# The position bias of the middle query chunks, computed per distance and written out in both directions

## Chip, core and metric

One core of one Trainium2 chip. The metric is the device time of one execution in microseconds. TensorE is called PE, VectorE DVE, ScalarE ACT, GpSimd POOL; SP is the engine that only issues transfers.

## The reference

Attention with a learned position bias, followed by two gated MLPs, all in float32:

```python
B, H, S, D = 4, 8, 576, 64; hidden = 32
scores = 1/sqrt(D) * q @ k.T
rel  = pos[:, None] - pos[None, :]
x    = log1p(|rel|) / log1p(max(pos[:, None], 1))
bias = relu(x * w1 + b1) @ w2                    # [S, S, H]
attn = softmax(scores + bias);  y = attn @ v      # 2304 tokens x 512
h1   = (sigmoid(y @ w_gate) * (y @ w_val)) @ w_out          # d_ff 1536
h    = h1 @ w_in;  out = (h * clip(h + 3, 0, 6) / 6) @ w_out2   # d_ff 2048
```

For a fixed query row i the bias depends on the key column j through the distance |i - j| alone; the row itself enters as a scale, 1/log1p(max(i, 1)).

## The kernel before

The 576 query rows are cut into five chunks `QC`: four of 128 rows and one of 64. For each chunk the attention of all batches and heads is computed, then the two MLPs run over its tokens (512, in the last chunk 256) in 68 steps of twelve matmuls of up to 512 columns. The attention of chunk c+1 and its bias are interleaved with the MLP steps of chunk c. This is called block c: `block(0)` to `block(4)`. What precedes block 0 is the lead: the bias and the attention of chunk 0, and the first two groups of the bias of chunk 1. In block 0 the MLP weights are also converted and split for the first time (lines L470 to L486), four DVE and two ACT operations a step; later blocks reload them (`wp<-wsp`).

The bias is computed in groups G of 16 query rows, 36 in all. `bias_hidden` makes the hidden layer of a group as four tiles `z` of 128 partitions (4 rows x 32 hidden units) by 576 key columns. Each is one instruction that scales a slice of the position table `tz_t`, adds b1 and applies the relu: two on ACT (L128), two on DVE (L130). The table holds log1p|j - i| for every offset, and the slice's start sets the rows. `bias_mm` (L139) multiplies by `w2`: eight matmuls of 288 columns, four column tiles of PE side by side for each half, into a PSUM buffer `ps` of two banks (pool `s1`, two buffers, also used by the scores of attention). `bias_out` empties it into `bo`, on ACT (L155) except in chunk 0 (DVE, L157), and after two groups a transfer (L165) writes them to `biasD`, one DRAM tensor a chunk, laid out rows x heads x columns. `bias_read` (L179) reads two heads of a chunk as `bm`. The scores of a pair of units are `pair_qk` (L372), and the sum with `bm` and its minimum `pair_min` (L394); chunks 0 and 1 use L235 and L250.

Where events lie is written by hand in fractions of MLP steps (`block_events`, `chunk_bias`). The order on PE is the program's everywhere; in the lead also that of ACT, DVE and SP, in block 0 also that of SP. The other orders are set by a planner at compile time, which may also draw an instruction of block 0 on DVE into the lead. Dependencies and their waits come from the compiler.

Of the kernel before, what the change touches and what calls it, by code (L numbers as in the profile page):

```python
# [25 lines left out]
NC = len(QC)  # L26
NQ = 128
NTOK = B * NQ
NT = 320
WA = 5  # L30
# [26 lines left out]
def fused_kernel(ctx: ExitStack, tc: tile.TileContext, qd, kd, vd, tz, rd, zc, w2b, iden, wpack, out):  # L57
# [26 lines left out]
    biasD = [dr_p.tile([n, H, S], F32, name=f"biasD{c}") for c, (_, n) in enumerate(QC)]  # L84
# [9 lines left out]
    t0 = S - QC[0][1]  # L94
    nc.sync.dma_start(out=tz_t[:, t0:], in_=tz[:, t0:])
# [24 lines left out]

    def bias_hidden(G, g):

        if g == 0:
            z_q[G] = z_p.tile([128, 4, S], F32, name="z")
        t = 4 * G + g
        z, x = z_q[G][:, g], tz_t[:, S - 4 - 4 * t:2 * S - 4 - 4 * t]
        if g < 2:
            nc.scalar.activation(out=z, in_=x, func=AF.Relu, scale=sc_t[:, t:t + 1], bias=b1c)  # L128
        else:
            nc.vector.tensor_scalar(  # L130
                out=z, in0=x, scalar1=sc_t[:, t:t + 1], scalar2=zc_t[:, 2:3], op0=ALU.mult, op1=ALU.max
            )

    def bias_mm(G):
        z = z_q.pop(G)
        ps = bo_q[G] = s_ps()
# [8 lines left out]

    def bias_out(G, x=0, last=True):
# [3 lines left out]
        if x == 0:  # L150
            bo_t[0] = A["bo"].tile([128, 2, S], F32, name="bo")
# [21 lines left out]
    def bias_read(u):  # L173
        c, hp, b = u
        n = QC[c][1]
        if b == 0:
            bm = bm_p.tile([128, 2, S], F32, name="bm")
            for p in range(0, NQ, n):
                nc.sync.dma_start(out=bm[p:p + n], in_=biasD[c][:, 2 * hp:2 * hp + 2, :])  # L179
# [391 lines left out]
    with ExitStack() as lead:  # L571
# [5 lines left out]
        nc.sync.dma_start(out=tz_t[:, 0:t0], in_=tz[:, 0:t0])  # L577
# [5 lines left out]
        for G in range(NG0 + NG1 + 1):  # L583
# [6 lines left out]
            if G and G != NG0:  # L590
                bias_out(G - 1, (G - 1) % 2, G % 2 == 0)
        for u in us[1:3]:
            load_v(u)
# [43 lines left out]
    def chunk_bias(c, t0, dt, done=0):  # L637
# [6 lines left out]
        for g in range(0, nG, 2):  # L644
            def outs(G=G0 + g, two=min(2, nG - g)):
                for i in range(two):
                    bias_mm(G + i)
                for i in range(two):
# [75 lines left out]
    def block_events(k):  # L724
        ev = []
        last = NSTEP - 1
        if k == 0:
            ev += chunk_bias(1, 2.0, 1.5, NG1)
# [6 lines left out]
        elif k == 2:  # L735
            d = (last - 9.5 - 0.5) / 7
            ev += chunk_pairs(3, 0.5, d, d, last)
# [32 lines left out]
def _positions():  # L770
# [4 lines left out]
    return num.astype(np.float32), (1.0 / den).astype(np.float32)  # L775


def _layout(q, k, v, w1, b1, w2, moe_w_gate, moe_w_val, moe_w_out, moe2_w_in, moe2_w_out):
# [12 lines left out]
    tz, rd = _positions()  # L791
# [19 lines left out]
    return dict(qd=qd, kd=kd, vd=vd, tz=tz, rd=rd, zc=zc, w2b=w2b, iden=np.eye(128, dtype=np.float32), wpack=wpack.view(np.uint64).reshape(NSTEP, 128, 512))  # L811
# [19 lines left out]
```

## Time and profile before

| | |
|---|---|
| median of 3 runs | 1117.78 us (1116.67 to 1118.62) |
| profiled execution | 1116.91 us |
| its span, first to last instruction | 1115.1 us |
| PE busy | 1101.9 us, 99% |
| DVE busy | 664.2 us, 60% |
| ACT busy | 538.7 us, 48% |
| bias matmuls L139 | 576 records, two for each matmul |

The span is what the trace shows; the execution's own time has 1.8 us around it. Matmuls are pipelined and their ends modelled, so a busy PE is not necessarily PE at its peak. Busy shares are means over stages that have different limits. The granted clock of PE was 1.00 of full speed throughout.

### The profile page before, as it was taken

The numbers are of one execution on the slowest core, as the hardware profiler recorded it, in microseconds if no ns is written. First come the engines' busy times: TensorE is split into PE (matmuls) and PEld (weight loads), VectorE is DVE, ScalarE is ACT, GpSimd is POOL, SyncE is SP. The second block draws the span as 40 slices with busy tenths as digits, with TensorE's granted clock in tenths as the row PEclk, the third lists the DMA queues.
The fourth block names the chain that finished last, engine by engine and source line by source line (L and its number), as shares of the span: only waits on it lengthen the run. The fifth ranks groups of instructions, "written<-read, shape, count | busy, mean of one in ns | idle before, by whom it ended". The sixth has DMA issues, their size and how long they took to land.

```text
span 1115.1 us, 20239 instructions
## 1 busy us (share of the span) xinstructions
PE 1101.9 (99%) x7334; PEld 890.3 (80%) x7334; DVE 664.2 (60%) x1517; ACT 538.7 (48%) x1062; POOL 126.0 (11%) x240
## 2 busy tenths in 40 slices
PE   8999999999999999999999999999999999999998
PEld 4777777777777787777888787888878787879998
DVE  7999998898963455796815653756342407052232
ACT  7887887788863633664503442444132205131231
POOL 1000000000010002112131111111340202031000
PEclk9999999999999999999999999999999999999999
DMA  6947999989986579999997878887897978768997
GB/s 220 361 179 268 373 390 402 391 284 372 395 299 229 196 256 284 272 309 293 288 322 257 267 259 269 255 275 243 276 289 243 261 241 251 239 206 303 364 371 272
DMA packets 117267, 321.26 MB, mean 288 GB/s; under 512 B 20656, under 2 KB 29360, under 8 KB 117168
## 3 DMA queue, kind: packets, MB, share of 16 engines
q1 hardware_dynamic: 107136, 298.89, 78.0%
q0 software_dynamic: 8512, 20.72, 6.7%
q8 instruction: 59, 0.97, 0.3%
q10 hardware_dynamic: 1520, 0.35, 0.2%
q14 instruction: 40, 0.33, 0.1%
HBM read 244.73 MB, written 50.99 MB: 265 GB/s over the span
## 4 chain that ended last, share of the span: by engine, by line
PE 83%; DVE 6%; ACT 6%; issue 2%; DMA 2%; SPq 1%; ACTq 0%; DVEq 0%
PE ps L500 66%; PE ps L330 7%; PE ps L139 3%; PE ps L286 2%; PE ps L372 2%; PE ps L235 2%; ACT z L128 1%; DVE wp L481 1%; ACT cm L470 1%; ACT bo L155 1%; DVE cm L475 1%; DMA kt<-kd 1%; PE ps L378 1%; DVE cm L472 1%; ACT s L260 1%
## 5 line engine op out<-in xcount | busy, mean ns | idle before, releaser
L500 PE MATMUL ps<-xyh,wp 128*128 128x512 f32 (+1 forms) x1600 | 466.6, 371 | 1.2 <-ACT xyh L350 0.8
L500 PEld LDWEIGHTS ps<-xyh,wp 128*128 128x128 f32 x1600 | 290.1, 189 | 59.5 <-issue 3.5
L500 PE MATMUL ps<-gh,wp 128*128 128x512 f32 (+1 forms) x1120 | 329.5, 372 | 0.2 <-ACT pT L289 0.2
L500 PE MATMUL ps<-xyl,wp 128*128 128x512 f32 (+1 forms) x800 | 295.1, 369 | 0.3 <-DVE xyl L513 0.3
L500 PEld LDWEIGHTS ps<-gh,wp 128*128 128x128 f32 x1120 | 203.4, 189 | 36.9 <-issue 2.0
L500 PE MATMUL ps<-gl,wp 128*128 128x512 f32 (+1 forms) x560 | 206.5, 369 | 0.0
L500 PEld LDWEIGHTS ps<-xyl,wp 128*128 128x128 f32 x800 | 150.9, 189 | 24.6 <-DVE xyl L513 0.8
L509 ACT ACTIVATE gh<-tmp 128x512 fp32r<-128x512 f32 (+1 forms) x140 | 82.2, 588 | 148.6 <-DVE tmp L531 107.4
L309 POOL DMA_DIRECT2D pT<-t x192 | 94.4, 499 | 506.7 <-DVE t L299 161.5
L260 ACT ACTIVATE s<-s,m 128x576 f32<-128x576 f32 x144 | 110.4, 769 | 22.6 <-DVE m L394 13.3
L500 PEld LDWEIGHTS ps<-gl,wp 128*128 128x128 f32 x560 | 105.7, 189 | 16.7 <-DVE gl L511 0.5
L511 DVE TENSOR_TENSOR gl<-tmp,gh 128x512 fp32r<-128x512 f32 (+1 forms) x140 | 88.4, 634 | 46.7 <-ACT gh L509 45.9
L531 DVE SCALAR_TENSOR_TENSOR tmp<-tmp,ps 128x512 f32<-128x512 f32 (+1 forms) x60 | 37.8, 631 | 97.6 <-PE ps L500 97.0
L330 PEld LDWEIGHTS ps<-pT,vt 128*64 128x64 f32 x1600 | 79.2, 137 | 16.9 <-issue 14.9
L330 PE MATMUL ps<-pT,vt 128*64 128x128 f32 (+1 forms) x1600 | 92.0, 266 | 0.4 <-issue 0.3
L537 DVE SCALAR_TENSOR_TENSOR tmp<-tmp,ps 128x512 f32<-128x512 f32 (+1 forms) x80 | 50.0, 629 | 53.4 <-ACT tmp L536 51.9
L561 POOL DMA_DIRECT2D outT<-acc x40 | 28.1, 756 | 365.5 <-DVE acc L552 346.1
L350 ACT ACTIVATE xyh<-ps 128x128 fp32r<-128x128 f32 (+1 forms) x52 | 16.4, 316 | 108.7 <-PE ps L330 108.7
L351 DVE TENSOR_TENSOR xyl<-ps,xyh 128x128 fp32r<-128x128 f32 (+1 forms) x52 | 17.7, 341 | 80.5 <-ACT xyh L350 80.2
L536 ACT ACTIVATE tmp<-ps 128x512 f32<-128x512 f32 (+1 forms) x80 | 43.8, 548 | 42.0 <-PE ps L500 39.5
L527 ACT ACTIVATE tmp<-ps 128x512 f32<-128x512 f32 (+1 forms) x60 | 33.1, 552 | 57.4 <-PE ps L500 57.2
L128 ACT ACTIVATE z<-tz_t,zc_t,sc_t 128x576 f32<-128x576 f32 x72 | 57.8, 857 | 1.5 <-DVE sc_t L106 1.2
(65 smaller groups left out, 1108.2 us busy)
## 6 DMA issues: line engine op xcount, KB each, us to landing
wp<-wsp SPq DMA_DIRECT2D x272, 512.0 KB, 5.1
wd<-wpack SPq DMA_DIRECT2D x68, 512.0 KB, 6.8
wsp<-wp SPq DMA_DIRECT2D x68, 512.0 KB, 5.8
vt<-vd SPq DMA_DIRECT2D x80, 320.0 KB, 5.1
kt<-kd SPq DMA_DIRECT2D x80, 288.0 KB, 5.2
pT<-t POOLq DMA_DIRECT2D x192, 72.0 KB, 4.8
pT<-t SPq DMA_DIRECT2D x128, 72.0 KB, 4.6
bm<-biasD SPq DMA_DIRECT2D x15, 576.0 KB, 6.0
```

The lines of the kernel that those rows point to most:

```text
L128: nc.scalar.activation(out=z, in_=x, func=AF.Relu, scale=sc_t[:, t:t + 1], bias=b1c)
L139: nc.tensor.matmul(out=ps[32 * g:32 * g + 32, j, 0:NI], lhsT=w2b_t, rhs=z[:, g, NI * j:NI * j + NI], start=True, stop=True, tile_position= ...
L260: nc.scalar.activation(out=s[:, h], in_=s[:, h], func=AF.Exp, scale=-1.0, bias=d["m"][:, h:h + 1], accum_out=r[:, h:h + 1],)
L309: (nc.sync if p[0][0] < 4 and i > 1 else nc.gpsimd).dma_start(out=pt[32 * q:32 * q + 32, i].rearrange("j u t i -> j (u t i)"), in_=t[32 * ...
L330: nc.tensor.matmul(out=po[64 * h:64 * h + 64, n * a:n * a + n], lhsT=vt[:, v], rhs=pt[:, m * a:m * a + m, k, :], start=(t == 0), stop=(t = ...
L500: nc.tensor.matmul(out=ps[:, 0:nt], lhsT=w[:, c, :], rhs=x[:, 0:nt], start=(first and c == 0 and i == 0), stop=(last and c == 3 and i == 2),)
L509: nc.scalar.activation(out=hi[:, 0:nt], in_=src, func=AF.Copy, scale=scale)
L511: nc.vector.tensor_tensor(out=lo[:, 0:nt], in0=src, in1=hi[:, 0:nt].bitcast(F32), op=ALU.subtract)
L527: nc.scalar.activation(out=th, in_=ps, func=AF.Tanh, scale=0.5)
L531: nc.vector.scalar_tensor_tensor(out=th, in0=th, scalar=1.0, in1=ps, op0=ALU.add, op1=ALU.mult)
L536: nc.scalar.activation(out=t, in_=ps, func=AF.Relu, bias=3.0)
L537: nc.vector.scalar_tensor_tensor(out=t, in0=t, scalar=6.0, in1=ps, op0=ALU.min, op1=ALU.mult)
```

## The change

In chunks 1 to 3 (groups 8 to 31) the hidden layer and its product are computed over the distance d = |i - j| instead of over the key column. For a pair of groups that starts at row i0 of 576, distances up to the larger of i0 + 31 and 575 - i0 are needed, n = 320 to 512 values instead of 576. `bias_hidden` reads a table of log1p(d), `td`, that is the same on all partitions; it is held in the first 512 columns of `tz_t`, whose old content there is loaded again at the start of block 2 for chunk 4. `bias_mm` makes four matmuls of n columns in place of eight of 288. The two groups of a pair take the two banks of one PSUM buffer.

`bias_out2` empties both groups together: ACT writes distances 0 to 575 - i0 forwards into the right part of `bo`, DVE writes distances 1 to i0 + 31 backwards (a step of -1) into the left part. A row of `bo` is then 607 columns, the same window for all 32 rows of the pair. Two transfers on SP (16 rows each) put it into a DRAM tensor laid out heads x rows x 703. `bias_read` shifts each row to its own place by reading with a row step of 702, so that row r begins one element earlier than row r-1 did; it reads two pieces of 2,304 bytes for each row where it read one of 4,608. Chunks 0 and 4 are as before.

```diff
--- before.py
+++ after.py
@@ -27,6 +27,8 @@
 NQ = 128
 NTOK = B * NQ
 NT = 320
+SW = S + NQ - 1
+SU = S + 31
 WA = 5
 WB = 3
 YG, OG = 3, 2
@@ -54,7 +56,7 @@
 
 
 @with_exitstack
-def fused_kernel(ctx: ExitStack, tc: tile.TileContext, qd, kd, vd, tz, rd, zc, w2b, iden, wpack, out):
+def fused_kernel(ctx: ExitStack, tc: tile.TileContext, qd, kd, vd, tz, td, rd, zc, w2b, iden, wpack, out):
     nc = tc.nc
     PS = bass.MemoryType.PSUM
 
@@ -81,7 +83,10 @@
         return m1.tile([128, 512], F32, name="ps")
 
 
-    biasD = [dr_p.tile([n, H, S], F32, name=f"biasD{c}") for c, (_, n) in enumerate(QC)]
+    biasD = [
+        dr_p.tile([H * n * SW] if 0 < c < NC - 1 else [n, H, S], F32, name=f"biasD{c}")
+        for c, (_, n) in enumerate(QC)
+    ]
     wsp = dr_p.tile([NSTEP, 128, 2, 512], F32, name="wsp")
 
     tz_t = const.tile([128, 2 * S - 4], F32, name="tz_t")
@@ -92,6 +97,7 @@
     w2b_t = const.tile([128, 32], F32, name="w2b_t")
     id_t = const.tile([128, 128], F32, name="id_t")
     t0 = S - QC[0][1]
+    td_t = tz_t[:, 0:512]
     nc.sync.dma_start(out=tz_t[:, t0:], in_=tz[:, t0:])
     nc.scalar.dma_start(out=zc_t[:, 0:2], in_=zc)
     nc.scalar.dma_start(out=sc_t, in_=rd)
@@ -118,12 +124,25 @@
 
     A, z_q, bo_q = {}, {}, {}
 
+    def mirrored(G):
+        return QC[1][0] <= 16 * G < QC[NC - 1][0]
+
+    def reach(G):
+
+        i0 = 16 * (G & ~1)
+        left, right = i0 + 31, S - 1 - i0
+        return left, right, max(left, right) + 1
+
     def bias_hidden(G, g):
 
         if g == 0:
             z_q[G] = z_p.tile([128, 4, S], F32, name="z")
         t = 4 * G + g
-        z, x = z_q[G][:, g], tz_t[:, S - 4 - 4 * t:2 * S - 4 - 4 * t]
+        if mirrored(G):
+            n = reach(G)[2]
+            z, x = z_q[G][:, g, 0:n], td_t[:, 0:n]
+        else:
+            z, x = z_q[G][:, g], tz_t[:, S - 4 - 4 * t:2 * S - 4 - 4 * t]
         if g < 2:
             nc.scalar.activation(out=z, in_=x, func=AF.Relu, scale=sc_t[:, t:t + 1], bias=b1c)
         else:
@@ -133,6 +152,16 @@
 
     def bias_mm(G):
         z = z_q.pop(G)
+        if mirrored(G):
+            if G % 2 == 0:
+                bo_q[G] = s_ps()
+            ps, n = bo_q[G & ~1], reach(G)[2]
+            for g in range(4):
+                nc.tensor.matmul(
+                    out=ps[32 * g:32 * g + 32, G % 2, 0:n], lhsT=w2b_t, rhs=z[:, g, 0:n],
+                    start=True, stop=True, tile_position=(0, 32 * g),
+                )
+            return
         ps = bo_q[G] = s_ps()
         for j in range(2):
             for g in range(4):
@@ -143,12 +172,33 @@
 
     bo_t = {}
 
+    def bias_out2(G):
+
+        ps = bo_q.pop(G)
+        c = 16 * G // NQ
+        i0 = 16 * G - QC[c][0]
+        left, right, _ = reach(G)
+        bo = A["bo"].tile([128, 2, SU], F32, name="bo")
+        nc.scalar.activation(
+            out=bo[:, :, left:], in_=ps[:, :, 0:right + 1], func=AF.Identity, scale=D ** 0.5, bias=cv_t
+        )
+        nc.vector.tensor_scalar(
+            out=bo[:, :, left - 1::-1], in0=ps[:, :, 1:left + 1],
+            scalar1=D ** 0.5, scalar2=cv_t, op0=ALU.mult, op1=ALU.add,
+        )
+        at = NQ - 32 - i0
+        rows = biasD[c].rearrange("(h r w) -> r h w", h=H, w=SW)[i0:i0 + 32, :, at:at + SU]
+        for x in range(2):
+            nc.sync.dma_start(
+                out=rows[16 * x:16 * x + 16], in_=bo[:, x],
+            )
+
     def bias_out(G, x=0, last=True):
 
         ps = bo_q.pop(G)
         c = min(G // 8, NC - 1)
         if x == 0:
-            bo_t[0] = A["bo"].tile([128, 2, S], F32, name="bo")
+            bo_t[0] = A["bo"].tile([128, 2, SU], F32, name="bo")[:, :, 0:S]
         bo = bo_t[0][:, x]
         bv = bo.rearrange("p (a j) -> p a j", a=2)
         if c:
@@ -175,8 +225,12 @@
         n = QC[c][1]
         if b == 0:
             bm = bm_p.tile([128, 2, S], F32, name="bm")
-            for p in range(0, NQ, n):
-                nc.sync.dma_start(out=bm[p:p + n], in_=biasD[c][:, 2 * hp:2 * hp + 2, :])
+            if 0 < c < NC - 1:
+                rows = biasD[c].rearrange("(h x) -> h x", h=H)[2 * hp:2 * hp + 2, NQ - 1:NQ - 1 + NQ * (SW - 1)]
+                nc.sync.dma_start(out=bm, in_=rows.rearrange("h (r w) -> r h w", w=SW - 1)[:, :, 0:S])
+            else:
+                for p in range(0, NQ, n):
+                    nc.sync.dma_start(out=bm[p:p + n], in_=biasD[c][:, 2 * hp:2 * hp + 2, :])
             bm_q[c, hp] = bm
 
     def load_rows(u, bias=True):
@@ -574,7 +628,7 @@
         lead.enter_context(tc.manual_schedule(engines={ET.PE, ET.Activation, ET.DVE, ET.SP}))
         load_rows(us[0], False)
         load_k(us[0])
-        nc.sync.dma_start(out=tz_t[:, 0:t0], in_=tz[:, 0:t0])
+        nc.sync.dma_start(out=tz_t[:, 0:t0], in_=td[:, 0:t0])
         load_k(us[1])
         load_v(us[0])
         nc.sync.dma_start(out=id_t, in_=iden)
@@ -587,8 +641,10 @@
                 for g in range(4):
                     bias_hidden(G, g)
                 bias_mm(G)
-            if G and G != NG0:
+            if G and G < NG0:
                 bias_out(G - 1, (G - 1) % 2, G % 2 == 0)
+            if G == NG0 + NG1:
+                bias_out2(NG0)
         for u in us[1:3]:
             load_v(u)
         att_qk(us[0])
@@ -645,6 +701,9 @@
             def outs(G=G0 + g, two=min(2, nG - g)):
                 for i in range(two):
                     bias_mm(G + i)
+                if mirrored(G):
+                    bias_out2(G)
+                    return
                 for i in range(two):
                     bias_out(G + i, i, i == two - 1)
             ev.append((t0 + dt * g + dt + 1, outs))
@@ -725,6 +784,7 @@
         ev = []
         last = NSTEP - 1
         if k == 0:
+            ev.append((1.0, lambda: nc.sync.dma_start(out=td_t[:, t0:], in_=td[:, t0:])))
             ev += chunk_bias(1, 2.0, 1.5, NG1)
             ev += chunk_att(1, 15.5, last, 2)
         elif k == 1:
@@ -734,6 +794,8 @@
             ev += chunk_bias(3, 19.99 + 1.5 * d, d / 2)
         elif k == 2:
             d = (last - 9.5 - 0.5) / 7
+            n4 = 2 * S - 4 - 4 * 16 * 8
+            ev.append((0.1, lambda: nc.sync.dma_start(out=tz_t[:, 0:n4], in_=tz[:, 0:n4])))
             ev += chunk_pairs(3, 0.5, d, d, last)
             ev += chunk_bias(4, d - 0.51, d)
         elif k == 3:
@@ -772,7 +834,8 @@
     q = np.tile(np.arange(4), 32)[:, None]
     num = np.log1p(np.abs(np.arange(2 * S - 4)[None] - (S - 4) - q).astype(np.float32))
     den = np.log1p(np.maximum(4 * np.arange(S // 4)[None] + q, 1).astype(np.float32))
-    return num.astype(np.float32), (1.0 / den).astype(np.float32)
+    dist = np.log1p(np.arange(512).astype(np.float32))[None].repeat(128, 0)
+    return num.astype(np.float32), dist.astype(np.float32), (1.0 / den).astype(np.float32)
 
 
 def _layout(q, k, v, w1, b1, w2, moe_w_gate, moe_w_val, moe_w_out, moe2_w_in, moe2_w_out):
@@ -788,7 +851,7 @@
     w2b = np.zeros((128, 32), np.float32)
     for g in range(4):
         w2b[g::4, 8 * g:8 * g + 8] = w2
-    tz, rd = _positions()
+    tz, td, rd = _positions()
     wpack = np.empty((NSTEP, 128, 4, 128), moe_w_gate.dtype)
 
     def col(w, f):
@@ -808,7 +871,7 @@
             wpack[i] = blk(moe_w_out, s[1], s[2])
         else:
             wpack[i] = blk(moe2_w_out, s[1], s[2])
-    return dict(qd=qd, kd=kd, vd=vd, tz=tz, rd=rd, zc=zc, w2b=w2b, iden=np.eye(128, dtype=np.float32), wpack=wpack.view(np.uint64).reshape(NSTEP, 128, 512))
+    return dict(qd=qd, kd=kd, vd=vd, tz=tz, td=td, rd=rd, zc=zc, w2b=w2b, iden=np.eye(128, dtype=np.float32), wpack=wpack.view(np.uint64).reshape(NSTEP, 128, 512))
 
 
 # ---- launch: one core ----
```

## Rows read from the trace of the kernel before

**Rows 1.** Busy by stage: start:end us, busy of PE, PEld, DVE, ACT, POOL; clock, DMA, GB/s.

```profile
84.50:147.40 62.90, 61.70 (x342) 45.59 (x340) 58.98 (x111) 50.62 (x84) 0.00 (x0) 1.00 0.92 332
130.00:142.00 12.00, 11.73 (x53) 8.61 (x51) 11.93 (x24) 8.02 (x15) 0.00 (x0) 1.00 1.02 388
337.50:542.20 204.70, 201.92 (x1320) 158.82 (x1322) 123.96 (x292) 103.11 (x185) 25.18 (x50) 1.00 0.82 266
542.20:1115.10 572.90, 567.75 (x3748) 481.59 (x3748) 247.79 (x581) 171.20 (x346) 93.16 (x176) 1.00 0.84 273
545.00:560.00 15.00, 15.00 (x80) 12.17 (x76) 14.27 (x36) 8.33 (x17) 3.75 (x8) 1.00 1.00 305
```

**Rows 2.** The chain that ended last: start us, us, what.

```profile
30.17 8.52 DMA kt<-kd
...
353.59 2.08 PE ps L139 x32
...
444.66 1.22 PE ps L372 x16
```

**Rows 3.** Order of time, 442 to 447.5: start, us, engine, line, operation, idle before.

```profile
442.51 2.15 PE L139 MATMUL ps<-z,w2b_t 128*32 128x288 f32 x32
...
442.63 0.38 ACT L350 ACTIVATE xyh<-ps 128x256 fp32r<-128x256 f32 x1 [7.19 <-PE ps L330]
...
443.04 0.42 DVE L351 TENSOR_TENSOR xyl<-ps,xyh 128x256 fp32r<-128x256 f32 x1 [6.33 <-ACT xyh L350]
...
443.75 0.74 ACT L155 ACTIVATE bo<-ps,cv_t 128x576 f32<-128x576 f32 x1 [0.74 <-PE ps L139]
443.76 2.05 DVE L130 TENSOR_SCALAR z<-tz_t,sc_t,zc_t 128x576 f32<-128x576 f32 x4 [0.29 <-PE ps L139]
444.39 1.62 ACT L128 ACTIVATE z<-tz_t,zc_t,sc_t 128x576 f32<-128x576 f32 x2
...
445.91 0.72 ACT L155 ACTIVATE bo<-ps,cv_t 128x576 f32<-128x576 f32 x1
...
446.69 0.41 PE L372 MATMUL ps<-kh,qh 64*128 64x320 f32 x2 [0.68 <-ACT bo L155]
```

**Rows 4.** Waits, 337 to 560: engine line waited for, us, times, longest.

```profile
PE ps L372 <- ACT bo L155: 2.8, 4, 0.7
```

**Rows 5.** Instructions by line and shape: busy us, mean ns, idle before.

```profile
L250 DVE CUSTOM_DVE_ANT_0 s<-ps,bm 128x576 f32<-128x576 f32 x64 | 46.6, 753 | 4.9 <-PE ps L235 4.8
...
L130 DVE TENSOR_SCALAR z<-tz_t,sc_t,zc_t 128x576 f32<-128x576 f32 x72 | 37.6, 575 | 6.0 <-PE ps L139 5.6 <-issue 0.3
...
L155 ACT ACTIVATE bo<-ps,cv_t 128x576 f32<-128x576 f32 x28 | 20.5, 731 | 10.5 <-PE ps L139 10.5
...
L157 DVE TENSOR_SCALAR bo<-ps,cv_t 128x576 f32<-128x576 f32 x8 | 6.5, 812 | 1.2 <-PE ps L139 1.2
...
L106 DVE TENSOR_SCALAR sc_t<-sc_t,zc_t 128x144 f32<-128x144 f32 x1 | 0.3, 295 | 0.0
```

**Rows 6.** Order of time, 19 to 25, the end of the lead's bias.

```profile
20.02 2.04 DVE L130 TENSOR_SCALAR z<-tz_t,sc_t,zc_t 128x576 f32<-128x576 f32 x4
...
24.08 0.39 SPq L165 DMA_DIRECT2D biasD<-bo  x1
...
24.10 1.23 PE L235 MATMUL ps<-kt,qt 64*128 64x288 f32 x6 [0.15 <-ACT bo L155]
```

**Rows 7.** Order of time on PE, 104 to 147.

```profile
142.18 0.73 PE L500 MATMUL ps<-xyh,wp 128*128 128x512 f32 x2 [0.45 <-DVE wp L481]
```

**Rows 8.** DMA issues: count, KB each, median us to landing.

```profile
bm<-biasD SPq DMA_DIRECT2D x15, 576.0 KB, 6.0
biasD<-bo SPq DMA_DIRECT2D x14, 576.0 KB, 3.8
...
tz_t<-tz SPq DMA_DIRECT2D x1, 350.0 KB, 3.3
```

## Prediction

> **What bounds the kernel now.** I read the busy times by stage first, then the chain that ended last, then the moment-by-moment view around the bias work, because a change of this kind is worth what the stage it sits in lets through. By stage [rows 1], TensorE (PE) has work for nearly all of every stretch, so the whole kernel is bound there. The one stretch with a second candidate is 84.5 to 147.4 us, where the bias of chunk 1 runs beside the conversion of the MoE weights: VectorE (DVE) is busy 58.98 of 62.90 us, in its last part 11.93 of 12.00, and at 142.18 PE, out of prepared weights, waits 0.45 us for DVE [rows 7]. In the chain [rows 2] the bias matmuls of chunks 2 and 3, all in block 1, stand as eight pieces, one for each pair of groups, six of 2.08 us and two cut short where the chain goes over to ACT; the rest of that part is nearly all matmuls. The close view of one of the last four pairs [rows 3] shows a wait behind it: the score matmuls that follow need the PSUM buffer that ScalarE (ACT) is still emptying; PE stands 0.68 us, in all four 2.8 us [rows 4].
>
> **PE, the saving.** A group's product takes 288 columns eight times now; two records each, 32 for a pair, in 2.08 us [rows 2], four column tiles side by side. Afterwards there are four products of n columns, n being 448, 416, 384, 352 in chunk 1 (by pairs), 320, 320, 352, 384 in chunk 2 and 416, 448, 480, 512 in chunk 3. I scale by columns: a pair costs 2.08 x n/576, so 1.16, 1.16, 1.27, 1.39 in chunk 2 and 1.50, 1.62, 1.73, 1.85 in chunk 3. Saved: 3.35 us in chunk 2, 1.62 in chunk 3, and 2.08 in the three pairs of chunk 1 inside block 0. Fewer, longer instructions could only save a little more; if instead side-by-side tiles fell out of step nothing would be saved, but nothing in the rows suggests it. Block 1 has PE busy 201.92 of 204.70 us [rows 1], so all 4.97 us count there.
>
> **The eviction, the new cost.** Before, each group is emptied by ACT alone, 731 ns [rows 5], each into its own PSUM buffer. Now both groups of a pair share one buffer, ACT empties the right part, 2(right+1) elements, DVE the mirrored left part, 2 left elements, and the buffer is free when both are done. The trace has no place where the two engines read one PSUM buffer independently. The bounds are side by side, or one behind the other. The nearest rows are ACT's and DVE's reads of one buffer at 442.63 and 443.04 [rows 3], where DVE starts after ACT ends; that is a data dependence, but I take this end. The Trainium skill (PSUM — Partial Sum Buffer, PSUM bank collisions raise a hardware error) says the hardware does not arbitrate two engines that read the same bank and partitions at once, so software must order them; no run here shows it. By that rule the sum below is the serial one, -3.1 us; without it -7.6.
>
> Prices: ACT 731 ns at 576 elements [rows 5] and 0.38 us at 256 [rows 3] give 1.10 ns an element; DVE reading PSUM, 753 ns at 576 [rows 5] and 0.42 us at 256 [rows 3], 1.04 ns, from 812 ns at 576 for this very operation [rows 5]. A reversed write is not in the trace; I give it the forward price and bound it in the rivals.
>
> *Chunk 3.* Counted from the first bias matmul of the pair, using G=24: the first group ends at 0.75, ACT begins 0.13 later (as at 443.75 [rows 3]), but with the next pair's two hidden tiles, which wait only for the first group (DVE's begin at the same moment in [rows 3]); 0.76 us each now (444.39 to 445.91), at 448 columns 0.62, until 2.12. Then 320 elements, 0.45 us, to 2.57; DVE, whose own four tiles are done by then, takes 830 elements, 1.08 us, to 3.70. PE reaches the matmul that needs the buffer at 1.50 + 1.22 [rows 2] = 2.72 and stands until 3.76: 1.04 us. The same working gives 1.04, 1.06 and, for the last pair, before which no hidden tile lies since chunk 4's input is not back yet, 0.61. Together 3.75 against 2.8 now [rows 4]: +0.95 us. Side by side DVE would start at about 1.75 and the four waits would be about 0.2 each: -2.0.
>
> *Block 0.* ACT gets lighter: four hidden tiles a pair shortened by 160, 192, 224 columns, 2.5 us, and six evictions of 731 ns against three of 1.01, 0.94, 0.87, another 1.6. DVE gets 382, 446 and 510 elements, 0.61 + 0.68 + 0.74 = 2.0 us, and its hidden tiles, 575 ns at 576 columns and, by the 295 ns of another scaling at 144 [rows 5], 0.65 ns a column, give back 1.5: +0.5 us on the engine that PE waits for at 142.18 [rows 7]. In-order DVE may also stand behind ACT's half, at most 2.8 us; against this, some of DVE's 3.9 us of idle time [rows 1] is waiting for ACT, which is lighter. Bounds -2.1 (all of PE's saving) and +3.3; I take 0. The 2.08 us of PE are then lost, as PE would only arrive earlier at DVE.
>
> *Lead.* Groups 8 and 9 end the bias of the lead. DVE's four tiles from 20.02 [rows 6] shrink from 2.04 to 1.71 us, and the last product, no longer in two halves, ends near 22.6. Then ACT takes 896 elements, 1.08 us, DVE 318, 0.54 us, so the buffer is free at 24.5, where the scores got theirs at 24.10. The write behind it is issued at 24.5, not 24.08, and is two transfers, 0.39 us more on SP [rows 6]; queued behind are the value and key loads, one of which ends the chain's wait at 38.7 [rows 2]. Between +0.4 (compute) and +0.8 (loads): +0.6 us. Side by side +0.1.
>
> **DMA.** The position table now shares its tile with the distances, so 318 KB are loaded again at the start of block 2; the like transfer landed in 3.3 us [rows 8]. Chunk 4 needs it seven steps later, but from 545 to 560 the DMA engines are busy throughout, at 305 GB/s [rows 1], by which 318 KB are 1.0 us: 0 to 1.0, taken as +0.3. The 64 columns loaded in block 0 are 33 KB, nothing. The bias reads, 6.0 us to landing [rows 8], become 256 rows of 2,304 bytes for 128 of 4,608; even doubled they are issued one pair or two units ahead, over 12 us: hidden, and exposed by up to 6 us a read if that lead were lost. The two writes of a pair land in 3.8 us [rows 8], steps before their reader.
>
> **Sum:** lead +0.6, block 0 0, chunk 2 -3.35, chunk 3 -1.62 + 0.95, table +0.3: **-3.1 us**, so 1113.8 for the profiled execution, whose own time was 1116.91. The median is 0.87 higher, and I state the prediction against it: 1114.7. After block 1 PE is busy 567.75 of 572.90 us [rows 1], so what is gained before reaches the end.
>
> **Rivals.**
> *The two halves overlap* (or the compiler orders the queues so that DVE goes first): lead +0.1, block 0 -1.0, chunks 2 and 3 -4.97, waits -2.0, table +0.3: -7.6, 1110.2. For it: nothing in the program text links the two reads. Against: above. 22%.
> *The two writes of a pair are chained.* They interleave in one tensor, 16 rows of each of eight heads; if they are taken as overlapping, SP stands 3.8 us [rows 8] in the lead with the key loads behind it, and PE with them by up to 3.4 us: 1118. In blocks 0 and 1 weights are loaded five steps ahead, which covers it. Writes of disjoint, unmixed rows did not wait before. 10%, no change.
> *The reversed write is slow* (ends slower). 318 + 1,338 + 3,704 = 5,360 elements lie where something waits. At one extra ns each the change costs +5.4 instead, 1120.1; it decides at about 0.6 ns extra (no gain) and 1.0 ns (slower by 0.2%). For it: no row has a negative step. Against: DVE reads PSUM at 1.04 ns whatever else it does. 10%.
> *Engine orders.* From block 1 on only PE's order is written out; other durations give other queues, in either direction by a few us. 8%.
>
> **Chances.** A measurement of this kernel tells about 0.2%, 2.2 us. The forecast (50%) is spread by some 2 us: 0.35 faster, 0.14 same, 0.01 slower. Overlap: 0.22 faster. Chained: 0.07 same, 0.03 slower. Slow write: 0.10 slower. Orders: 0.03, 0.02, 0.03. Together 0.60, 0.23, 0.17. The range runs from overlap with half of block 0's remaining 1.1 us and a better order, 1109, to the slow write, 1120; the likeliest alone is 1112.5 to 1117.
>
> **What would show it.** Bias matmuls: 16 records a pair, 1.16 us at 320 columns and 1.85 at 512. DVE's eviction beginning only where ACT's ends; if they overlap, the first rival. DVE at 1.08 us for 830 elements; if 1.9 or more, the third. In block 1, PE waits for DVE's eviction at the four scores after it, about 1 us each. At 142 us PE still waits for DVE. In the lead the second write issued right behind the first; if 3.8 us later, the second rival. I would be wrong most likely where DVE stands in its queue: block 0, where my bounds are 5.4 us apart.

## The result: slower by 0.8%

The changed kernel takes 1127.09 us in the median of six runs (1126.06 to 1128.38); the kernel before took 1118.22 beside it (1116.67 to 1120.49). The ratio is 1.0079, interval 1.0067 to 1.0091. Forecast were 1114.7 us, a range of 1109 to 1120 and a chance of 0.17 for slower. The profiled execution took 1126.06 us with a span of 1124.3, 9.2 longer than before's.

To see where the time went, compare the same event in both traces. The products with v (`ps<-pT,vt`, 10 to 80 matmuls in a row) occur in the same order in every kernel here. The table gives how much later than in the kernel before such a product starts; the difference between two columns is what the stretch between them lost. The rows below the first are experiments, explained further down; in the last four a pair of chunk 3 (1.5 to 2.1 us) already lies ahead of the fourth point.

| start in the kernel before, us | 84.98, end of lead | 157.99 | 335.15, end of block 0 | 440.18, behind chunk 2's bias | 542.13, behind chunk 3's | 1008.00 |
|---|---|---|---|---|---|---|
| changed kernel | +13.18 | +12.94 | +12.08 | +9.12 | +9.26 | +8.66 |
| e9_one_column | +2.47 | +2.43 | +2.18 | -0.78 | -0.65 | -0.78 |
| e5_pair_early | +1.83 | +1.40 | +1.29 | +0.13 | -6.11 | -5.57 |
| e6_before_pair_early | +0.09 | +0.14 | +0.17 | +2.47 | -2.85 | -3.46 |
| e11_two_psum_tiles | +0.22 | +0.43 | +1.20 | +0.04 | -6.20 | -5.91 |
| e12_chunk1_plain | -0.01 | -0.32 | -0.04 | -1.20 | -7.44 | -7.39 |

So the loss is in the lead, all of it in the first 50 us, and the rest of the kernel gives back some 4.5 us. The chain of the changed kernel, of which the longest pieces are shown, has four in the lead that before's lacks: PE's work hangs on transfers `bm<-bo`, 10.1 us together.

```profile
9.18 2.03 DMA bm<-bo
14.42 3.60 DMA bm<-bo
21.19 2.25 DMA bm<-bo
26.66 2.23 DMA bm<-bo
30.27 2.30 PE ps L160 x12
...
39.01 2.96 PE ps L289 x8
```

DVE's waits between 0 and 60 us say who waits for them: L207, the line that empties a group of chunk 0 (L157 before). The kernel before has no such wait.

```profile
DVE bo L207 <- DMA bm<-bo: 10.0, 4, 3.3
```

In order of time, with the idle time in brackets: the first group of a pair is emptied at 7.70, its rows leave through L213 (`bm<-bo`) from 8.55 on, and the second group, which goes into the other half of the same tile `bo`, is emptied only at 11.34, once those transfers have landed. PE then stands at its PSUM buffer.

```profile
7.70 0.82 DVE L207 TENSOR_SCALAR bo<-ps,cv_t 128x576 f32<-128x576 f32 x1 [0.66 <-PE ps L168]
...
8.55 6.53 SPq L213 DMA_DIRECT2D bm<-bo  x6
...
11.34 0.82 DVE L207 TENSOR_SCALAR bo<-ps,cv_t 128x576 f32<-128x576 f32 x1 [1.84 <-DMA bm<-bo]
...
12.30 3.04 PE L168 MATMUL ps<-z,w2b_t 128*32 128x288 f32 x26 [1.59 <-DVE bo L207]
```

Windows of the changed kernel (start:end, length, busy PE, PEld, DVE, ACT, POOL, granted clock, DMA, GB/s) show a second, smaller part: after the gaps PE's granted clock is 0.70 of full speed from 30 to 44 us, where it was 1.00 in the kernel before. The eight score matmuls at 39.01 in the chain took 2.96 us, those at 28.03 in the kernel before 1.91 (second fence). The next three stages answer to [rows 1]: in block 0 DVE is busy 59.70 of 63.30 us and still close to the bound, the rest of block 0 has PE busy throughout, and in block 1 PE lacks 4.5 of 184.50 us, which are the waits shown below.

```profile
0.00:30.00 30.00, 19.43 (x154) 10.15 (x154) 15.17 (x30) 16.77 (x22) 2.69 (x7) 0.94 0.45 151
30.00:44.00 14.00, 12.15 (x45) 6.93 (x45) 9.70 (x27) 5.25 (x11) 0.74 (x1) 0.70 0.73 242
...
97.00:160.30 63.30, 61.58 (x303) 45.35 (x302) 59.70 (x114) 47.22 (x82) 0.00 (x0) 1.00 0.91 330
160.30:349.00 188.70, 188.18 (x1152) 147.26 (x1152) 163.11 (x344) 146.89 (x296) 4.21 (x6) 1.00 0.97 361
349.00:533.50 184.50, 180.02 (x1078) 140.14 (x1074) 116.31 (x267) 86.05 (x160) 21.16 (x42) 1.00 0.84 267
```

```profile
28.03 1.91 PE L235 MATMUL ps<-kt,qt 64*128 64x288 f32 x8 [0.39 <-DVE m L250]
```

Of the 13.2 us, 9.3 have been lost when the last bias product ends (23.20 before, 32.48 after). From there to the first product with v the kernel before took 10.4 us, the changed one 14.7; e5_pair_early, which has the same instructions there at a granted clock of 1.00, took 11.9. So about 1.4 us are the new eviction and the loads behind it, and about 2.9 the clock.

From block 1 on the profile looks much as forecast. The chain has chunk 2's four pairs, and the first of chunk 3, as 16 matmuls where there were 32 in 2.08 us [rows 2]:

```profile
365.68 1.21 PE ps L160 x16
...
375.32 1.21 PE ps L160 x16
...
384.96 1.32 PE ps L160 x16
...
394.70 1.43 PE ps L160 x16
...
451.70 1.53 PE ps L160 x16
```

A pair of chunk 3 in order of time, the counterpart of [rows 3]: the products, the next hidden tiles, ACT's half, DVE's half, and PE, which waits for the latter.

```profile
451.63 1.60 PE L160 MATMUL ps<-z,w2b_t 128*32 128x416 f32 x16
...
452.61 1.42 ACT L147 ACTIVATE z<-tz_t,zc_t,sc_t 128x448 f32<-128x448 f32 x2 [0.47 <-PE ps L160]
...
453.93 0.56 ACT L182 ACTIVATE bo<-ps,cv_t 128x384 f32<-128x384 f32 x1
...
454.53 1.08 DVE L185 TENSOR_SCALAR bo<-ps,cv_t 128x830 f32<-128x830 f32 x1
...
455.67 0.42 PE L426 MATMUL ps<-kh,qh 64*128 64x320 f32 x2 [1.08 <-DVE bo L185]
```

DVE begins at 454.53, 0.04 us after ACT has ended, and takes 1.08 us for 830 elements written backwards. The wait of PE behind it, between 349 and 545 us, stands for [rows 4]:

```profile
PE ps L426 <- DVE bo L185: 4.5, 4, 1.2
```

And the transfers, for [rows 8] (count, KB each, median us to landing):

```profile
bm<-biasD SPq DMA_DIRECT2D x15, 576.0 KB, 5.6
biasD<-bo SPq DMA_DIRECT2D x24, 303.5 KB, 4.5
...
tz_t<-tz SPq DMA_DIRECT2D x1, 318.0 KB, 5.6
```

### The profile page after: what moved, and what is told of

Read it like the earlier page. It is cut to its first block, busy times and chain, and to the rows that moved or that the text cites. A ratio compares the mean times of both kernels' runs of the same rounds, so it can differ in the third digit from the quotient of the medians.

```text
span 1124.3 us, 19865 instructions
## 1 busy us (share of the span) xinstructions
PE 1099.5 (98%) x7142; PEld 887.0 (79%) x7142; DVE 670.3 (60%) x1529; ACT 525.5 (47%) x1050; POOL 126.1 (11%) x240
## 4 chain that ended last, share of the span: by engine, by line
PE 90%; DVE 4%; DMA 3%; ACT 1%; issue 1%; SPq 0%; DVEq 0%; ACTq 0%
PE ps L554 72%; PE ps L384 7%; PE ps L289 3%; PE ps L340 3%; PE ps L426 2%; PE ps L160 1%; DVE z L149 1%; DMA bm<-bo 1%; DMA kt<-kd 1%; PE ps L432 1%; DMA wp<-wsp 1%; DMA biasD<-bo 0%; DVE bo L185 0%; ACT z L147 0%; DMA vt<-vd 0%
## 5 line engine op out<-in xcount | busy, mean ns | idle before, releaser
L384 PEld LDWEIGHTS ps<-pT,vt 128*64 128x64 f32 x1600 | 79.0, 137 | 16.2 <-issue 13.4
L147 ACT ACTIVATE z<-tz_t,zc_t,sc_t 128x576 f32<-128x576 f32 (+7 forms) x72 | 51.0, 763 | 19.4 <-PE ps L160 10.2
```

The costliest lines, as they stand in the source:

```text
L384: nc.tensor.matmul(out=po[64 * h:64 * h + 64, n * a:n * a + n], lhsT=vt[:, v], rhs=pt[:, m * a:m * a + m, k, :], start=(t == 0), stop=(t = ...
```

## Experiments on the lead: one tile's width

The diff changes one more thing in chunk 0, although its computation stays: `bo` grows from 576 to 607 columns a group, of which chunk 0 uses 576. The theory (A): this width makes the compiler take the second group's half as overlapping the first group's, which is still being read. The rival (B): the lead is late for what groups 8 and 9 do now, or for loads behind the two writes.

**e1_own_tile.** Chunk 0's evictions get a tile of their old width (pool `bo0`, three buffers; `bo` keeps one in the lead); the mirrored form stays.

```diff
-            bo_t[0] = A["bo"].tile([128, 2, SU], F32, name="bo")[:, :, 0:S]
+            bo_t[0] = (
+                A["bo0"].tile([128, 2, S], F32, name="bo0") if c == 0
+                else A["bo"].tile([128, 2, SU], F32, name="bo")[:, :, 0:S]
+            )
...
```

> The changed kernel, with the eviction tile of chunk 0 back to two rows of 576 columns in a pool of its own; all else as changed. Theory A: the whole loss is DVE's wait, in the lead, of each odd group's eviction for the transfers of the even group out of the same, now 1214 columns wide, tile (10.0 us in four waits, and about 2.6 us behind them while PE's granted clock was low). Then the lead ends some 12 us earlier than in the changed kernel, the four waits are gone, and the time is 1115 (1113.5 to 1116.5), 0.3% under before. Rival B: the lead lost its time to its own two mirrored groups (serial eviction of 896 and 318 elements, two writes on SP, loads behind them): then at most 3 us come back, 1124.

1116.6 us, ratio to the kernel before 0.9991 (0.9977 to 1.0005). DVE's wait for the transfers is gone, and 10.5 us with it.

**e2_before_wide.** The opposite: the kernel before, with nothing but the wide tile.

```diff
-            bo_t[0] = A["bo"].tile([128, 2, S], F32, name="bo")
+            bo_t[0] = A["bo"].tile([128, 2, S + 31], F32, name="bo")[:, :, 0:S]
```

> The kernel before, with only the eviction tile made 607 columns a row and its first 576 used; nothing else of the change. Theory A: DVE waits for transfers of chunk 0 as in the changed kernel, 4 times, 10 us, and the time is 1128 to 1131 (before plus 10 to 13). Rival B: no such wait, 1118.

1128.34 us, 1.0091 (1.0074 to 1.0108), and the same four waits of DVE (L157 is the line that empties chunk 0 there):

```profile
DVE bo L157 <- DMA bm<-bo: 10.2, 4, 3.5
```

One line of the diff alone costs more than the whole change does. A holds twice. B is out as the main cause: what it names can be no more than the 2.5 us by which e1_own_tile still leaves the lead late. What about the width does it?

**e9_one_column** has the changed kernel's tile one column wider, 608, and **e10_before_577** the kernel before's.

```diff
-        bo = A["bo"].tile([128, 2, SU], F32, name="bo")
+        bo = A["bo"].tile([128, 2, SU + 1], F32, name="bo")[:, :, 0:SU]
...
-            bo_t[0] = A["bo"].tile([128, 2, SU], F32, name="bo")[:, :, 0:S]
+            bo_t[0] = A["bo"].tile([128, 2, SU + 1], F32, name="bo")[:, :, 0:S]
```

```diff
-            bo_t[0] = A["bo"].tile([128, 2, S], F32, name="bo")
+            bo_t[0] = A["bo"].tile([128, 2, 577], F32, name="bo")[:, :, 0:S]
```

> The changed kernel with the eviction tile one column wider, 608 columns a group instead of 607 (the last one unused); chunk 0 still uses the wide tile. Theory A (the false wait of chunk 0's evictions comes from the row pitch: 607 x 4 = 2428 bytes is no multiple of 32, so the end of one group and the start of the next fall into one 32-byte piece and are taken as overlapping; 608 x 4 = 2432 is 76 x 32): the four waits for the transfers (10.0 us) go without any tile of chunk 0's own, first MLP step at 88.5 to 90, 1116.5 us as e1_own_tile. Theory B (it comes from the tile being wider than the part that chunk 0 uses): the waits stay, 1127 us.

> The kernel before with its eviction tile one column wider than before, 577 columns a group (2308 bytes, 72.1 pieces of 32) and nothing else. Theory A (row pitch): all of the loss of e2_before_wide by a single unused column, four waits of DVE for the transfers of about 10 us in all, 1128 us. Theory B (the width itself, more bytes a row): 31 columns cost 10 us, one costs nothing that can be measured, 1118 us.

e9: 1116.57 us, 0.9989 (0.9978 to 1.0), the wait is gone. e10: 1134.35 us, 1.0138 (1.0118 to 1.0158), the wait is there with a single unused column:

```profile
DVE bo L157 <- DMA bm<-bo: 10.4, 4, 3.7
```

The width counts, not how much wider it is. But the rule by pieces of 32 bytes (theory A of these two) did not survive: programs compiled for each width from 576 to 609, without a run, have the waits wherever the largest common factor of width and 576 is 4 or less, and lack them wherever it is 6 or more, whole pieces or not (theory C). Two runs tell the rules apart: **e13_after_612**, as e9 with `SU + 5`, and **e14_before_585**, as e10 with 585.

> The changed kernel with 612 columns a group in the eviction tile: 2448 bytes, 76.5 pieces of 32. Theory A (a row pitch in whole pieces of 32 bytes is what keeps chunk 0's evictions free of the wait): 612 is as bad as 607, DVE waits four times for the transfers, 10 us in all, 1127 us. Theory C (whether two strided pieces of the tile are told apart depends on a common factor of the pitch and the 576 columns in use: programs compiled for each width from 576 to 609 have the waits where that factor is 1 to 4 and lack them where it is 6 or more; 612 and 576 share 36): no such wait, 1116.6 us as e9_one_column (1115.5 to 1117.5).

> The kernel before with 585 columns a group in its eviction tile: 2340 bytes, 73.1 pieces of 32; 585 and 576 share 9. Beside e10_before_577 (share 1). Theory A (pieces of 32 bytes): slower like e10_before_577, by 10 to 16 us. Theory C (common factor): same as before, 1118 us, DVE without a wait for the transfers, although the tile is eight columns wider than in e10_before_577.

e13: 1123.25 us, 1.0044 (1.0032 to 1.0056). e14: 1125.57 us, 1.0074 (1.006 to 1.0088). Neither time is as either theory had it. The traces split the answer. No eviction of chunk 0 waits for `bm<-bo` in either kernel, and e14 leaves the lead 0.04 us ahead of the kernel before: on the wait, C is right and A is wrong. (The runs have the waits at 577 and 607, which share 1 with 576, and lack them at 585, 608 and 612, which share 9 or more; the line between 4 and 6 rests on the compiled programs.) But from block 0 on both kernels lose time in small steps, e14 +0.5 at 157.99, +3.0 at 542.13, +7.2 at 1008.00, and so does e10 (+11.7 at the end of the lead, +18.3 at 1008.00). The groups by shape (busy us, mean ns, idle) show where: the 512-column MLP matmuls whose other operand is `gh` or `gl` take 399 or 400 and 394 or 395 ns for 394 and 390, while those with `xyh` do not change. First the kernel before, then e14 (e10 has 400 and 395, e13 399 and 395):

```profile
L500 PE MATMUL ps<-xyh,wp 128*128 128x512 f32 x1280 | 408.6, 394 | 1.2 <-ACT xyh L350 0.8 <-DVE wp L481 0.4
...
L500 PE MATMUL ps<-gh,wp 128*128 128x512 f32 x896 | 288.7, 394 | 0.2 <-ACT pT L289 0.2
...
L500 PE MATMUL ps<-gl,wp 128*128 128x512 f32 x448 | 174.8, 390 | 0.0
```

```profile
L500 PE MATMUL ps<-xyh,wp 128*128 128x512 f32 x1280 | 408.8, 394 | 1.8 <-DVE wp L481 1.1 <-ACT xyh L350 0.8
L500 PE MATMUL ps<-gh,wp 128*128 128x512 f32 x896 | 293.8, 400 | 0.0
...
L500 PE MATMUL ps<-gl,wp 128*128 128x512 f32 x448 | 176.7, 394 | 0.0
```

That is 5.1 + 1.9 = 7.0 us in e14, nearly its whole loss. e13 loses as much against e9_one_column (from +3.3 at the end of the lead to +7.1, where e9 goes from +2.5 to -0.8). The tiles of `gh` are taken from SBUF behind `bo`, those of `xyh` ahead of it. If the two rows of a tile are rounded up to 32 bytes (taken so; no trace shows it), those of 577, 585 and 612 columns are 4640, 4704 and 4896 bytes, none a multiple of 64; those of 576, 607 and 608 are 4608, 4864 and 4864, all multiples, and kernels with these show no such loss. So where a tile lies within 64 bytes seems to cost these matmuls 4 to 6 ns; the addresses are not in the trace, and that reading is argued from six widths, not shown. Shown is that the width of `bo` goes with it.

## Experiments on the eviction

In all of these chunk 0 has the tile of e1_own_tile, with which they are compared.

**e3_by_group.** Each group of a pair is emptied by itself, ACT, DVE, ACT, DVE.

```diff
-        nc.scalar.activation(
-            out=bo[:, :, left:], in_=ps[:, :, 0:right + 1], ...
-        nc.vector.tensor_scalar(
-            out=bo[:, :, left - 1::-1], in0=ps[:, :, 1:left + 1], ...
+        for x in range(2):
+            nc.scalar.activation(
+                out=bo[:, x, left:], in_=ps[:, x, 0:right + 1], ...
+            nc.vector.tensor_scalar(
+                out=bo[:, x, left - 1::-1], in0=ps[:, x, 1:left + 1], ...
```

> e1_own_tile, with the mirrored eviction written per group: ACT right and DVE left of the first group, then of the second, four instructions where there were two. Theory: in chunk 3 the wait of PE behind the eviction (4.5 us in four waits in the changed kernel) comes from DVE's half standing behind ACT's half of both groups; per group, the first group's halves run while PE still multiplies the second, and the wait falls to under 2 us: 2.5 to 3.5 us faster than e1_own_tile, 1112. Rival: DVE's more instructions (0.2 us each) and its order in the queue eat it: within 1 us of e1_own_tile.

1133.45 us, 1.0146: 17 us worse than e1_own_tile, where 2.5 to 3.5 were to be gained. The first pair of chunk 3, in order of time:

```profile
443.68 0.65 DVE L186 TENSOR_SCALAR bo<-ps,cv_t 128x415 f32<-128x415 f32 x1
444.25 0.41 DVE L452 CUSTOM_DVE_ANT_0 s<-ps,bm 128x256 f32<-128x256 f32 x1
...
445.62 0.54 DVE L452 CUSTOM_DVE_ANT_0 s<-ps,bm,m 128x320 f32<-128x320 f32 x1
...
446.09 0.65 DVE L186 TENSOR_SCALAR bo<-ps,cv_t 128x415 f32<-128x415 f32 x1
...
446.88 0.41 PE L430 MATMUL ps<-kh,qh 64*128 64x320 f32 x2 [2.98 <-DVE bo L186]
...
448.99 0.63 PE L558 MATMUL ps<-gl,wp 128*128 128x512 f32 x1
```

Between DVE's two halves (443.68, 446.09) stand five of the minima of the scores (L452; 444.25 to 445.62): the planner has put them there, probably since the second half had to wait for ACT's. PE waits 2.98 us at 446.88, 12.5 us in the four pairs, and behind the gap its matmuls take 0.63 us (448.99) for 0.39, as the granted clock falls; 440 to 550 us has 0.92 of it and chunk 3 loses 15.9 us. Two more handovers on engines whose order is the planner's were worse than one long one.

**e7_engine_per_group** gives ACT both directions of the first group and DVE those of the second, which lie in different PSUM banks. **e8_both** adds the shift of e5 below.

```diff
-            out=bo[:, :, left:], in_=ps[:, :, 0:right + 1], ...
+            out=bo[:, 0, left:], in_=ps[:, 0, 0:right + 1], ...
...
-            out=bo[:, :, left - 1::-1], in0=ps[:, :, 1:left + 1],
+            out=bo[:, 1, left - 1::-1], in0=ps[:, 1, 1:left + 1],
...
+        nc.scalar.activation(
+            out=bo[:, 0, left - 1::-1], in_=ps[:, 0, 1:left + 1], ...
+        nc.vector.tensor_scalar(
+            out=bo[:, 1, left:], in0=ps[:, 1, 0:right + 1],
```

> e1_own_tile with the mirrored eviction shared out by group and not by side: ACT writes both sides of the pair's first group, DVE both sides of the second, each engine in a PSUM bank of its own, four instructions instead of two. The events of chunk 3 stay where they are. Theory A (the two halves stood one behind the other because both engines read the same two PSUM banks; in banks of their own they overlap): the pair's eviction falls from 1.7 us to about 1.1 us, the four waits of chunk 3 from 1.16 to about 0.6 us and the lead's from 1.0 to about 0.5 us, 2 to 3 us faster than e1_own_tile: 1114 us. Theory B (they stand in a row for another reason, a dependence through the eviction tile): four instructions in a row, 1.9 to 2.2 us, waits of 1.4 to 1.7 us, 1117 to 1119 us.

> e5_pair_early and e7_engine_per_group together. Theory A of both: chunk 3's waits are gone by the placement already, so only the lead gains 0.5 us (and up to 2 us more if its clock stays at 1.00) over e5_pair_early: 1110 to 1112 us. If e7's theory B holds, 1112 to 1114 us.

e7: 1134.17 us, 1.0148; e8: 1116.95, 0.9989 (0.9977 to 1.0002). The halves do not overlap: B is right on the row, but neither theory has either time. In the lead of e7 (order of time, idle in brackets) four instructions stand in a row, each waiting for the other engine's:

```profile
22.91 0.64 ACT L182 ACTIVATE bo<-ps,cv_t 128x448 f32<-128x448 f32 x1 [2.16 <-PE ps L160]
23.58 0.38 DVE L185 TENSOR_SCALAR bo<-ps,cv_t 128x159 f32<-128x159 f32 x1 [0.62 <-ACT bo L182]
24.00 0.39 ACT L189 ACTIVATE bo<-ps,cv_t 128x159 f32<-128x159 f32 x1 [0.45 <-DVE bo L185]
...
24.43 0.68 DVE L192 TENSOR_SCALAR bo<-ps,cv_t 128x448 f32<-128x448 f32 x1 [0.46 <-ACT bo L189]
...
25.25 0.51 PE L299 MATMUL ps<-kt,qt 64*128 64x288 f32 x2 [1.70 <-DVE bo L192]
```

In chunk 3 the last of them again falls behind the minima (PE waits 11.6 us in four), and block 0 loses 5.4 us, where PE waits 2.5 us for DVE's weights and 1.8 for ACT's; e8, with the pair early, has no wait in chunk 3 and is back at the time of e1, but 4.5 us above e5_pair_early, which differs from it in the eviction alone. It has lost that by the end of block 0 (+6.2 us at 335.15, e5 +1.3). In its lead PE waits 1.7 us, and its granted clock is 0.50 from 26 to 30 us and 0.54 from 30 to 36.

**e11_two_psum_tiles.** As e8, but with each group's product in a PSUM tile of its own.

```diff
-            if G % 2 == 0:
-                bo_q[G] = s_ps()
-            ps, n = bo_q[G & ~1], reach(G)[2]
+            ps, n = s_ps(), reach(G)[2]
+            bo_q.setdefault(G & ~1, []).append(ps)
```

> e5_pair_early with each group's product in a PSUM tile of its own (one bank of it used) instead of the two banks of one tile; ACT empties the first group, both directions, DVE the second. Theory A (in e7_engine_per_group the four evictions stood in a row across engines because both groups lie in one PSUM tile, though in two banks): here ACT and DVE work side by side, in the lead 22.9 to 24.0 us instead of 22.9 to 25.1, PE's wait there 0.3 to 0.5 us instead of 1.0 in e5_pair_early. The pair then holds both PSUM buffers, in chunks 2 and 3 as in the kernel before; with the pair early that is hidden: 1111 to 1113 us. Theory B (the row comes from the engines or from the eviction tile): 1.7 us wait in the lead as in e7_engine_per_group, 1113 to 1115 us.

1111.53 us, 0.9943 (0.9925 to 0.9961). Now the two engines can run beside each other, as at 385.6 us in chunk 2. In the lead they still come one after the other, as DVE is at its next hidden tiles until 23.2 us; but ACT starts at 22.27 where it started at 22.91 in e7, as it needs the first group's product alone, and nothing is handed over. PE's wait there is 0.32 us, and the lead ends 0.2 us late (e5: 1.8):

```profile
385.57 0.61 DVE L184 TENSOR_SCALAR bo<-ps,cv_t 128x383 f32<-128x383 f32 x1
385.67 0.57 ACT L188 ACTIVATE bo<-ps,cv_t 128x383 f32<-128x383 f32 x1
```

```profile
22.27 0.63 ACT L181 ACTIVATE bo<-ps,cv_t 128x448 f32<-128x448 f32 x1 [1.23 <-PE ps L159]
...
23.19 0.38 DVE L184 TENSOR_SCALAR bo<-ps,cv_t 128x159 f32<-128x159 f32 x1
...
24.31 1.21 PE L298 MATMUL ps<-kt,qt 64*128 64x288 f32 x6 [0.32 <-DVE bo L191]
```

The eviction tile, the four instructions and the backward writes are those of e8. So it is the shared PSUM tile that puts the engines in a row in e7 and e8, where each has a bank of its own.

**e4_chunk1_on_act.** In chunk 1 ACT writes the mirrored half too, since DVE is the engine that block 0 waits for [rows 1, 7].

```diff
+        if c == 1:
+            nc.scalar.activation(
+                out=bo[:, :, left - 1::-1], in_=ps[:, :, 1:left + 1], func=AF.Identity, ...
```

> e1_own_tile, with the mirrored left half of chunk 1 (three pairs in block 0, one in the lead) evicted by ACT too, 2.0 us less on DVE and 2.0 more on ACT. Theory: the early part of block 0 is bound by DVE, so PE's saving there is lost to DVE's new work; then this is 1 to 2 us faster than e1_own_tile, and PE does not wait for DVE's weight pieces where it did. Rival: block 0 is held by ACT or by transfers as much as by DVE: within 0.5 us or slower.

1118.93 us, 1.0005 (0.9993 to 1.0017): a miss. It is 2.3 us above e1_own_tile in the medians, which the intervals do not separate, where 1 to 2 us were to be gained. Up to 157.99 the kernel loses 2.4 us where e1_own_tile loses 0.2. PE's waits from 90 to 176 us say why: with 1.5 us of evictions at a time in front of it, ACT's step of the weight conversion is late, and DVE's with it (in e1_own_tile the two waits are 0.7 and 0.8 us).

```profile
PE ps L562 <- ACT wp L542: 2.6, 2, 1.3
PE ps L562 <- DVE wp L543: 1.5, 2, 1.0
```

## Experiments on the place: a version that beats both

**e5_pair_early** is e1_own_tile with chunk 3's bias two steps earlier, so that a pair's eviction lies beside MLP steps. **e6_before_pair_early** is the kernel before with the same edit.

```diff
-            ev += chunk_bias(3, 19.99 + 1.5 * d, d / 2)
+            ev += chunk_bias(3, 17.99 + 1.5 * d, d / 2)
```

> e1_own_tile with the bias events of chunk 3 two steps earlier, so that a pair's bias matmuls and its eviction lie among the MLP steps ahead of the chunk's scores. In e1_own_tile PE waits four times 1.16 us at the first score matmul behind a mirrored eviction (4.5 us in all, 440 to 510 us). Theory A (the serial eviction of a pair costs what is exposed behind it, and nothing else in chunk 3): the four waits go, the offsets of chunk 3 fall by 4 to 4.5 us, 1112.3 us (1111 to 1113.5). Theory B (the waits are only moved: the MLP step's PSUM tile or the bias matmuls in its middle wait instead): within 1 us of e1_own_tile, 1116 to 1117.

> The kernel before with the same two steps' shift of chunk 3's bias events, nothing else. It says how much of e5_pair_early's gain is the placement alone. Theory A: the four waits of 0.7 us (2.8 us in all) at the first score matmul go, 1115.4 us (1114.5 to 1116.5). Theory B: same as before, 1118.

e5: 1112.4 us, 0.9952 (0.9937 to 0.9968), as expected to 0.1. All four waits are gone; from 440 to 530 us PE is busy throughout:

```profile
440.00:530.00 90.00, 90.00 (x644) 71.10 (x643) 71.48 (x182) 49.92 (x98) 19.60 (x40) 1.00 0.95 300
```

e6: 1113.89 us, 0.9969 (0.9959 to 0.9979), 1.5 better than expected. Its four waits are gone too. Most of e5's gain is thus open to the kernel before as well; the mirrored form adds some 1.5 us to it, which the two intervals do not separate.

**e12_chunk1_plain.** e5_pair_early with chunk 1 as it was; `td` is loaded at step 30 of block 0.

```diff
-        return QC[1][0] <= 16 * G < QC[NC - 1][0]
+        return QC[2][0] <= 16 * G < QC[NC - 1][0]
```

> e5_pair_early with chunk 1 as in the kernel before (its hidden layer over columns, one direction, its DRAM tensor rows x heads x columns); chunks 2 and 3 stay mirrored. Theory A (the mirrored form of chunk 1 costs 1.2 to 1.8 us in the lead, gives 0.9 us back in block 0, and the gain is all in chunks 2 and 3: -3.0 and, with the pair early, -4.4): the offsets at the start of block 1 fall from +1.3 us to 0, the rest stays, 1110.5 us (1109.5 to 1112). Theory B (the early bias of block 0 is worth more than the lead costs): 1113 to 1115 us.

1111.65 us, 0.994 (0.9921 to 0.9958), theory A: in the table lead and block 0 are back at zero, and nearly all the gain lies in chunks 2 and 3. e5, e11 and e12 cannot be told apart by their intervals. Against e6_before_pair_early, the kernel before with the same placement, e12 is 2.2 us faster in the medians, and here the intervals just part (0.9958 and 0.9959). So much, barely separated, is the mirrored form worth in chunks 2 and 3 beside the placement. (Between the traces it is 3.9 us at 1008.00, but e12's trace is of the fastest of its six executions.)

## Why the prediction was wrong, point by point

- **Lead, +0.6: the step that failed**, +13.2 measured. It was worked out for groups 8 and 9 alone. The line of the diff that widens chunk 0's tile was put at nothing (the section on the change has chunk 0 "as before", which holds for its computation, not for its tile), and what it costs is a wait of DVE for transfers that stands in no term of the sum; 10.7 of the 13.2 us hang on it (the changed kernel against e9; e1 gives the same, and in e2 it alone makes the lead 11.9 us longer). The rival "two writes chained" feared the right kind of thing, a false overlap, in another place; the writes themselves went out back to back, two in 1.18 us at 34.21.
- **Groups 8 and 9.** The serial eviction was right: in e5 ACT's 1.01 us at 23.06, then DVE's 0.55 at 24.11, and PE's scores start at 24.71 for 24.10. But the lead ends 1.8 us late, not 0.4 to 0.8: the two writes hold SP for 1.18 us where 0.39 + 0.39 were assumed, the first key load behind them is issued at 27.30 us for 26.00, and PE's score matmuls wait 1.8 us for `kt`. In e11, where it is issued at 25.91, they wait 0.3 us.
- **Block 0, 0 taken between -2.1 and +3.3:** -1.1 in the changed kernel, -0.3 to -0.5 in e9, e1 and e5. Near the forecast; PE still waits for DVE's weights (1.4 us in the changed kernel). Of the 2.08 us that PE saves there, half or more are lost.
- **Chunk 2, -3.35:** -2.96. Scaling by columns was right to 5%: 1.21, 1.21, 1.32 and 1.43 us for the forecast 1.16, 1.16, 1.27 and 1.39.
- **Chunk 3, -0.67:** +0.14. The waits were 4.5 us, not 3.75: the last pair was given 0.61 us because no hidden tile was expected ahead of it, but chunk 4's are there and it waits like the others. The first pair's wait, 1.08 us for 1.04, was met with a wrong number in it: ACT's half was taken as 320 elements, 0.45 us, but G=24 has 2 x 192 = 384, 0.52 by the same price, measured 0.56. The first pair's product took 1.53 us (1.50).
- **Table, +0.3:** nothing. SP issued the load at 501.8 us, ahead of block 2; it landed in 5.6 us, and the offset falls by 0.6 between 542 and 1008 us.
- **Halves overlap, 22%:** no, in none of the twelve pairs, and the program text does link the two reads: they are of one PSUM tile. The Trainium skill (PSUM — Partial Sum Buffer, PSUM bank collisions raise a hardware error) wants two engines on one bank kept in order. e7 goes further than the rule: the compiler keeps them in order within one PSUM tile even where the banks differ; no run here has two engines read one bank at once.
- **Reversed write slow, 10%:** no, 1.08 us for 830 elements is what a forward read was forecast to take. **Bias reads** landed in 5.6 us for 6.0 in the median of 15, twelve of which have pieces half as long.

Without the tile's width the time would have been in the range: e9 has 1116.57 and e1 1116.6. But these are 1.1 and 1.6 us under the kernel before, with intervals that reach no change, for a forecast of 3.1: the lead is 2.5 us late for 0.6 and chunk 3 gains nothing for 0.7. In e1's lead the granted clock cost 1.5 us up to the first product with v (13.4 us from the last bias product, in e5 11.9); 0.6 of it is left at the lead's end, where e5 has waited for `kt`.

## What to carry to other kernels

Price every line of a diff at every place that runs it: a buffer made wider for one user changes what its other users wait for, without an instruction more. When a tile is shared by stages, look in the trace for waits of a writer on a reader of its other half, and give each user a tile of its own. A width with a large factor in common with the part in use removed the wait here too, but time it: 585 and 612 had no wait and lost 7 us elsewhere. An eviction is cheap where an MLP step covers it: placement gave more (3.7 us in e6) than fewer bias columns did beside it (1.5 us in e5, 2.2 in e12).

## What the runs showed of the hardware that was not expected

- A PE gap can cost more than itself, and does not always. In the lead of e9 and e1 a 1.0 us wait is followed by score matmuls at a granted clock of 0.50, the lower of PE's two levels (1.2 for 2.4 GHz); in e5, with the same instructions and the same wait there, the clock stays at 1.00, so the wait alone does not decide it. The windows of e1_own_tile, the wait in the first:

```profile
24.00:26.00 2.00, 1.23 (x6) 0.68 (x6) 1.02 (x2) 0.09 (x1) 0.00 (x0) 1.00 0.04 11
...
28.00:30.00 2.00, 2.00 (x6) 0.83 (x4) 1.42 (x3) 0.80 (x2) 0.00 (x0) 0.50 0.94 234
```

- The 512-column MLP matmuls took 394 or 400 ns with the size of an unrelated tile ahead of their operand, 7 us over the kernel; why is not shown.
